# One 256-token tile's first layers: the high and low parts of its tokens laid side by side as one operand of 512 columns

## The chip, the cores and the metric

The kernel runs on one core of a Trainium2 chip. The time is the device time of the whole program in microseconds (us), the median of some executions. One further execution was recorded by the hardware profiler; its rows are quoted below.

The core's engines run side by side, each its own list of instructions in the order in which the program wrote it: PE (TensorE, matrix multiply; its weight loads are the rows PEld), DVE (VectorE), ACT (ScalarE), POOL (GpSimd), and SP, which issues the transfers. They wait for each other by semaphores. PE writes to eight accumulation banks of 128 x 512 numbers (PSUM), and DVE or ACT must read a bank out before PE may use it for something else.

## What is computed

```python
x  = attention(q, k, v)                    # 2304 tokens of 512 numbers
P  = sinkhorn(exp(x @ w_gate))             # 2304 x 8
for e in range(8):                         # 512 -> 1024 -> 512
    out += P[:, e:e+1] * (relu(x @ w1[e]) @ w2[e])
r  = relu(out @ w_in)                      # 512 -> 2048
y  = (r * r) @ w_out                       # 2048 -> 512
```

All of it is in float32. The kernel multiplies with operands of a shorter form (`F32R`) and keeps the accuracy by splitting each number in a high part and a low part: a product is hi x hi + hi x lo + lo x hi, three matmuls.

## The kernel before

After the attention (up to some 126 us) the work is a list of 80 steps. A step handles 256 hidden columns. Steps 0 to 31 are the eight experts for the first part of the tokens and 32 to 63 the experts again for the rest; steps 64 to 71 and 72 to 79 are the last two lines of the reference in the same manner. In steps 0 to 31 and 64 to 71 the first part of the tokens is a pair of tiles of 512 tokens and one single tile of 256 tokens; in the other steps there is a pair alone.

In a step, `l1_pair` makes the first layer of the pair in seven units u1 to u7 (a unit is a function that writes some 1.4 us of PE work), `l2_units` the second layer of the step before in eight units for the pair and two for the single tile, and `l1_single` the first layer of the single tile, at the end of the step's list `order`. The order written by hand is u1 u2 u3 u4, then a unit of layer two and one of u5 u6 u7 in turn, then the rest of layer two, then the single tile. `run(u)` calls a unit and then whatever was put down for its place: `after(k, f)` puts f down for k units later, and `prep_w` puts down the splitting of the next weights (ACT copies the high part, L159, and DVE subtracts, L163). `narrow` turns one quarter of a block of 64-bit weights into float32 in a few DVE instructions (L274 to L296); its stages are written behind fixed places of `order` (2, 16, 17 and 1) in steps 2 to 29.

Names for the steps of the argument:

- `xs` holds the single tile's tokens, the high parts `xs_hi` and the low parts `xs_lo`, each 4 pieces (kc) of 128 x 256.
- `l1_single` makes, for each of two groups of 128 hidden columns (fc) and each kc, three matmuls of 256 columns (L754): hi weights by `xs_hi`, hi weights by `xs_lo`, lo weights by `xs_hi`. From step 3 on both fc share one bank `mm`, of which there are three, and are one unit.
- `evac_g` empties it into `sg`: in the expert steps ACT takes relu (L608) and DVE the low part (L601); in steps 64 to 71 there are four instructions (relu, square, high part, low part).
- In `l1_pair`, u1 is copied from bank `s` to bank `pt` by ACT (L705); u4 adds to `pt`, which ACT copies to `s2` (L717); only then may u5 add to `pt`, which ACT copies to `s3` (L721). DVE adds bank `xt` to `s3` (L722), after which u7 may add to `xt`.

```python
        def u4():
            product(bank_b, i, "sum", 1, 5)
            after(0, lambda: nc.scalar.copy(made["s2"], bank_b))

        def u5():
            product(bank_b, i, "sum", 2, 6)
            after(0, lambda: nc.scalar.copy(made["s3"], bank_b))
```

Of the kernel before, what the change touches and what calls it, by code (L numbers as in the profile page):

```python
# [10 lines left out]
F32 = mybir.dt.float32  # L11
F32R = mybir.dt.float32r
# [3 lines left out]
ALU = mybir.AluOpType  # L16
# [15 lines left out]
KC = DM // 128  # L32
FB = 256
FC = FB // 128
NCH = NTOK // 128
SPE = FE // FB
NS1 = E * SPE
NS2 = FF // FB
T = 512
NSG = 256  # L40
PAIRS = (0, 1280)
SINGLE = 1024
SCALED = 3
# [5 lines left out]
def tile_kernel(ctx: ExitStack, tc: tile.TileContext, a):  # L49
    nc = tc.nc  # L50
    out = a["out"]

    const = ctx.enter_context(tc.tile_pool(name="const", bufs=1))
    big = ctx.enter_context(tc.tile_pool(name="big", bufs=1))
# [11 lines left out]
    const.tile([128, 96], F32, name="pad_x")  # L66
    x_hi = big.tile([128, 7, 2, T], F32R, name="x_hi")
    x_lo = big.tile([128, 7, 2, T], F32R, name="x_lo")
    xs = big.tile([128, 4 + 2 * KC * NSG], F32R, name="xs")
    xs_hi, xs_lo = (xs[:, 4:].rearrange("p (h k n) -> p h k n", h=2, n=NSG)[:, h] for h in range(2))  # L70
    ptile = big.tile([128, NCH, E], F32, name="ptile")
    big.tile([128, 104], F32, name="pad_w")

    xf = xfp.tile([128, KC, NTOK], F32, name="xf")

# [14 lines left out]
    bufs = {"s": 2, "xt": 2, "pt": 1, "mm": 3}  # L90

    def bank(tag):
        return psum.tile([128, 512], F32, tag=tag, name=tag, bufs=bufs[tag])

    post = [None]

    def tmp(name):
        return post[0].tile([128, 512], F32, tag="tmp", name=name, bufs=3)
# [6 lines left out]
    wset = [None, None]  # L105
# [454 lines left out]
    g_t, acc = {}, {}  # L560
    turned = []
    gbuf, block, r32, own, l2_banks, spare = [], {}, [], {}, [], []
# [14 lines left out]
    def after(k, f):  # L577

        due.setdefault(clock[0] + k, []).append(f)
# [14 lines left out]
    def evac_g(i, ghi, glo, src, k):  # L594

        moe, s = steps[i]
        n = src.shape[-1]

        def low(z, relu):
            if relu:  # L600
                nc.vector.scalar_tensor_tensor(  # L601
                    out=glo, in0=z, scalar=0.0, in1=ghi.bitcast(F32), op0=ALU.max, op1=ALU.subtract
                )
            else:
                nc.vector.tensor_tensor(out=glo, in0=z, in1=ghi.bitcast(F32), op=ALU.subtract)

        if moe:
            after(k, lambda: nc.scalar.activation(out=ghi, in_=src, func=AF.Relu))  # L608
            after(k + 1, lambda: low(src, True))
            return  # L610
        held = {}

        def square():
            held["r"] = tmp("r")[:, :n]
            nc.scalar.activation(out=held["r"], in_=src, func=AF.Relu)

        def product():
            held["g"] = tmp("g")[:, :n]
            nc.vector.scalar_tensor_tensor(
                out=held["g"], in0=src, scalar=0.0, in1=held["r"], op0=ALU.max, op1=ALU.mult  # L620
            )

        after(k, square)
        after(k + 1, product)
        after(k + 2, lambda: nc.scalar.copy(ghi, held["g"]))
        after(k + 3, lambda: low(held["g"], False))
# [109 lines left out]
        return [u1, u2, u3, u4, u5, u6, u7]  # L736

    def l1_single(i):
        whole = []

        def unit(fcs):

            if fcs[0] == 0:
                whole[:] = [sg[:, h].rearrange("p (f n) -> p f n", f=FC) for h in range(2)]
                g_t[i, 1] = {(f, 0): tuple(z[:, f] for z in whole) for f in range(FC)}
            gh, gl = whole
            ps = (spare[0] if i == 2 * NS1 else bank("mm"))[:, :len(fcs) * NSG]
            hi, lo = wset[i % 2]["blk"]
            for n, fc in enumerate(fcs):
                k = 0  # L750
                for kc in range(KC):
                    c = slice((4 * fc + kc) * 128, (4 * fc + kc) * 128 + 128)
                    for w, z in ((hi, xs_hi), (hi, xs_lo), (lo, xs_hi)):
                        nc.tensor.matmul(  # L754
                            ps[:, n * NSG:n * NSG + NSG], w[:, c], z[:, kc], start=k == 0, stop=k == 3 * KC - 1
                        )
                        k += 1
            gh, gl = (g[:, fcs[0]:fcs[-1] + 1].rearrange("p f n -> p (f n)") for g in (gh, gl))
            evac_g(i, gh, gl, ps, 0)

        if i >= SCALED:
            return [lambda: unit(list(range(FC)))]
        return [lambda fc=fc: unit([fc]) for fc in range(FC)]

    def l2_units(i, which):

# [138 lines left out]
    with tc.manual_schedule():  # L905
# [7 lines left out]
        ps = psum.tile([128, 512], F32, tag="s", name="s")  # L913
# [158 lines left out]
        sg = post[0].tile([128, 2, FC * NSG], F32R, name="sg", bufs=1)  # L1072
# [32 lines left out]
        for i in range(len(steps) + 1):  # L1105
# [16 lines left out]
            l1 = l1_pair(i) if i else first_units  # L1122
            order = l1[:4] if i else l1[2:4]
            l1s = l1_single(i) if pair_of(i) == 0 else []
            if mixed(i - 1):
                v = l2_mixed(i - 1)
# [24 lines left out]
            if i + 1 in first[1:]:  # L1151
                c = first[1:].index(i + 1)
# [116 lines left out]
```

## Time and profile before

| | us |
|---|---|
| median of 3 executions | 1944.39 (1944.38 to 1948.22) |
| the profiled execution | 1944.46 |
| its span, first to last instruction | 1942.7 |
| PE busy | 1921.6 (99%) |
| DVE busy | 1627.4 (84%) |
| ACT busy | 747.0 (38%) |
| POOL busy | 636.5 (33%) |

The time of an execution is 1.8 us more than the span, which lies before the first and behind the last instruction. A row of the trace reads: start in us from the span's start, length in us, engine, line of the kernel, operation, what it writes <- what it reads, shape; in brackets how long the engine stood idle before it, and for whom. The end of a PE row is modelled and overlaps the next row, so the distance from one start to the next tells what a matmul costs. Rows of DVE and ACT also overlap a little: the next one starts some 0.1 us before the last ends.

### The profile page before, as it was taken

Reading aid. Unit: us, or ns where it says so; the run is one execution under the profiler, and the core shown is the slowest. Engines: PE = TensorE matmul, PEld = TensorE weight load, DVE = VectorE, ACT = ScalarE, POOL = GpSimd, SP = SyncE. Lnnn points to the kernel's source line nnn. Section 1 sums busy time; section 2 is a strip of 40 time slices with the busy share of each in tenths; the row PEclk is TensorE's granted clock in tenths of the full one; section 3 lists DMA queues with packets and bytes.
Section 4 is the critical chain, followed back from the end, with each engine's and each line's share of the span. In section 5 each row is a group of like instructions: output and inputs, shape, how many; then the busy total and the mean of one; then the engine's idle time right before and its main releaser. Section 6 shows DMA issues by size and latency. Waiting matters only on the chain.

```text
span 1942.7 us, 29441 instructions
## 1 busy us (share of the span) xinstructions
PE 1921.6 (99%) x11050; PEld 1601.8 (82%) x11050; DVE 1627.4 (84%) x2337; ACT 747.0 (38%) x1238; POOL 636.5 (33%) x556
## 2 busy tenths in 40 slices
PE   8999999999999999999999999999999999999999
PEld 7778888888888888888888888888888878888887
DVE  5868888888888888888578999998999987785897
ACT  3544433333333333333243333433333355443443
POOL 4633332333432223333033332423233343331231
PEclk9999999999999999999999999999999999999999
DMA  7655776766666656556977676667566777779661
GB/s 263 212 217 201 275 270 243 266 253 243 237 260 260 239 227 249 222 220 247 382 288 266 249 268 250 255 258 269 200 260 249 301 289 262 263 277 394 227 250 66
DMA packets 166399, 491.84 MB, mean 253 GB/s; under 512 B 17248, under 2 KB 40176, under 8 KB 166256
## 3 DMA queue, kind: packets, MB, share of 16 engines
q1 hardware_dynamic: 166256, 489.96, 67.6%
q8 instruction: 87, 1.43, 0.3%
q14 instruction: 56, 0.46, 0.1%
HBM read 281.15 MB, written 208.74 MB: 252 GB/s over the span
## 4 chain that ended last, share of the span: by engine, by line
PE 94%; DVE 4%; issue 1%; ACT 1%; DMA 0%; POOL 0%; SPq 0%; DVEq 0%; ACTq 0%; POOLq 0%
PE mm L783 28%; PE pt L570 16%; PE s L570 11%; PE xt L570 11%; PE mm L866 10%; PE mm L754 6%; PE s L866 4%; PE xt L866 4%; PE xt L443 1%; PE mm L976 1%; PE s L391 1%; DVE acc L880 1%; PE pt L428 1%; DMA w2l<-w_w2l 0%; PE mm L477 0%
## 5 line engine op out<-in xcount | busy, mean ns | idle before, releaser
L783 PE MATMUL mm<-w2h,g 128*128 128x512 f32 x1312 | 405.7, 391 | 0.0
L805 DVE SCALAR_TENSOR_TENSOR acc<-mm,ptile,acc 128x512 f32<-128x512 f32 x290 | 216.8, 748 | 104.1 <-PE mm L783 103.8
L783 PEld LDWEIGHTS mm<-w2h,g 128*128 128x128 f32 x1312 | 245.0, 188 | 49.9
L783 PE MATMUL mm<-w2l,g 128*128 128x512 f32 x656 | 255.5, 390 | 0.0
L682 POOL TENSOR_TENSOR r<-mix,r 128x512 f32<-128x512 f32 x39 | 51.2, 1313 | 541.6 <-DVE mix L671 428.8
L653 DVE TENSOR_TENSOR g<-r,g 128x512 fp32r<-128x512 f32 x156 | 158.6, 1017 | 47.2 <-ACT g L650 45.5
L177 POOL TENSOR_TENSOR sums<-raw 128x256 f32<-128x256 f32 x40 | 32.7, 819 | 489.3 <-DVE suml L163 446.1
L650 ACT CAST g<-r 128x512 fp32r<-128x512 f32 x156 | 96.8, 621 | 130.2 <-PE mm L866 109.7
L880 DVE TENSOR_TENSOR acc<-mm,acc 128x512 f32<-128x512 f32 x226 | 144.7, 682 | 0.0
L783 PEld LDWEIGHTS mm<-w2l,g 128*128 128x128 f32 x656 | 123.2, 188 | 25.8
L570 PE MATMUL s<-x_hi,blkh 128*128 128x512 f32 x320 | 125.4, 392 | 1.1 <-ACT pt L705 1.1
L570 PE MATMUL pt<-x_hi,sumh 128*128 128x512 f32 x320 | 124.9, 390 | 0.6 <-ACT s L717 0.6
L570 PE MATMUL xt<-x_hi,sumh 128*128 128x512 f32 x320 | 124.8, 390 | 0.0
L570 PE MATMUL s<-x_lo,blkh 128*128 128x512 f32 x320 | 124.8, 390 | 0.0
L570 PE MATMUL s<-x_hi,blkl 128*128 128x512 f32 x320 | 124.7, 390 | 0.0
L570 PE MATMUL xt<-x_hi,suml 128*128 128x512 f32 x320 | 124.6, 389 | 0.0
L570 PE MATMUL pt<-x_lo,sumh 128*128 128x512 f32 x320 | 124.6, 389 | 0.0
L570 PE MATMUL pt<-x_hi,suml 128*128 128x512 f32 x320 | 124.6, 389 | 0.0
L570 PE MATMUL xt<-x_lo,sumh 128*128 128x512 f32 x320 | 124.6, 389 | 0.0
L608 ACT ACTIVATE sg<-mm 128x512 fp32r<-128x512 f32 (+1 forms) x35 | 19.7, 562 | 272.8 <-PE mm L754 272.8
L754 PE MATMUL mm<-xs,blkh 128*128 128x256 f32 x640 | 115.8, 280 | 0.0
L608 ACT ACTIVATE g<-s 128x512 fp32r<-128x512 f32 x96 | 59.6, 621 | 136.5 <-DVE s L722 69.1
(224 smaller groups left out, 4810.7 us busy)
## 6 DMA issues: line engine op xcount, KB each, us to landing
raw<-in_w SPq DMA_DIRECT2D x61, 512.0 KB, 6.3
blkh<-w_blkh SPq DMA_DIRECT2D x41, 512.0 KB, 3.6
blkl<-w_blkl SPq DMA_DIRECT2D x41, 512.0 KB, 4.4
sumh<-w_sumh SPq DMA_DIRECT2D x41, 512.0 KB, 4.7
suml<-w_suml SPq DMA_DIRECT2D x41, 512.0 KB, 5.7
w_blkh<-blkh SPq DMA_DIRECT2D x40, 512.0 KB, 6.1
w_blkl<-blkl SPq DMA_DIRECT2D x40, 512.0 KB, 6.5
w_sumh<-sumh SPq DMA_DIRECT2D x40, 512.0 KB, 6.5
```

The lines of the kernel that those rows point to most:

```text
L177: tt(out=c(sums, 0), in0=c(raw1, 2), in1=c(raw1, 3), op=ALU.add)
L391: nc.tensor.matmul(ps[QB * head:QB * head + QB, 2 * (g % 3) + g // 3, :], qt[rows, pr, g * QB:g * QB + QB], kt[rows, pr, g * QB:g * QB + K ...
L570: nc.tensor.matmul(ps, w[:, c], z[:, x, j], start=start and k == 0, stop=stop and k == 5, skip_group_check=True)
L608: after(k, lambda: nc.scalar.activation(out=ghi, in_=src, func=AF.Relu))
L650: after(k, lambda: nc.scalar.copy(b[:, 0], src))
L653: lambda: nc.vector.tensor_tensor(out=b[:, 1], in0=src, in1=b[:, 0].bitcast(F32), op=ALU.subtract),
L682: sub = lambda o, x, y: nc.gpsimd.tensor_tensor(out=o, in0=x, in1=y, op=ALU.subtract)
L754: nc.tensor.matmul(ps[:, n * NSG:n * NSG + NSG], w[:, c], z[:, kc], start=k == 0, stop=k == 3 * KC - 1)
L783: nc.tensor.matmul(ps, g[:, c0 * 128:c0 * 128 + 128], wt[:, fc], start=k == 0, stop=k == 3 * FC - 1)
L805: nc.vector.scalar_tensor_tensor(out=dst, in0=ps, scalar=p, in1=dst, op0=ALU.mult, op1=ALU.add)
L866: nc.tensor.matmul(ps, w[wt][:, c], z[:, g], start=start and k == 0, stop=stop and k == 2, skip_group_check=True)
L880: nc.vector.tensor_tensor(out=o, in0=ps, in1=o, op=ALU.add)
```

## The change

`xs` is laid out so that for each kc the high and the low part stand side by side: one operand of 512 columns. For steps 0 to 31 and 65 to 71, each fc is now a unit of its own with a bank of its own. For each kc there is one matmul of 512 columns, hi weights by both parts, and one of 256, lo weights by `xs_hi`, which adds to the bank's left half. The product is then the sum of the two halves: ACT copies the right half to `s3` (256 columns), and DVE adds the left half to it. `s3` is the same buffer that `l1_pair` uses. When both fc are done, `evac_g` reads `s3` instead of the bank, and is put down two units later than before. Step 64 keeps its three matmuls, in `one_bank`. Two spare columns move from `xs` to `pad_w`.

```diff
--- before.py
+++ after.py
@@ -66,10 +66,10 @@
     const.tile([128, 96], F32, name="pad_x")
     x_hi = big.tile([128, 7, 2, T], F32R, name="x_hi")
     x_lo = big.tile([128, 7, 2, T], F32R, name="x_lo")
-    xs = big.tile([128, 4 + 2 * KC * NSG], F32R, name="xs")
-    xs_hi, xs_lo = (xs[:, 4:].rearrange("p (h k n) -> p h k n", h=2, n=NSG)[:, h] for h in range(2))
+    xs = big.tile([128, KC, 2, NSG], F32R, name="xs")
+    xs_hi, xs_lo = (xs[:, :, h] for h in range(2))
     ptile = big.tile([128, NCH, E], F32, name="ptile")
-    big.tile([128, 104], F32, name="pad_w")
+    big.tile([128, 108], F32, name="pad_w")
 
     xf = xfp.tile([128, KC, NTOK], F32, name="xf")
 
@@ -736,31 +736,53 @@
         return [u1, u2, u3, u4, u5, u6, u7]
 
     def l1_single(i):
-        whole = []
-
-        def unit(fcs):
-
-            if fcs[0] == 0:
-                whole[:] = [sg[:, h].rearrange("p (f n) -> p f n", f=FC) for h in range(2)]
-                g_t[i, 1] = {(f, 0): tuple(z[:, f] for z in whole) for f in range(FC)}
-            gh, gl = whole
-            ps = (spare[0] if i == 2 * NS1 else bank("mm"))[:, :len(fcs) * NSG]
+        whole, halves = [], []
+
+        def set_out():
+            whole[:] = [sg[:, h].rearrange("p (f n) -> p f n", f=FC) for h in range(2)]
+            g_t[i, 1] = {(f, 0): tuple(z[:, f] for z in whole) for f in range(FC)}
+
+        def flat(h):
+            return whole[h].rearrange("p f n -> p (f n)")
+
+        def columns(fc, kc):
+            return slice((4 * fc + kc) * 128, (4 * fc + kc) * 128 + 128)
+
+        def one_bank():
+            set_out()
             hi, lo = wset[i % 2]["blk"]
-            for n, fc in enumerate(fcs):
-                k = 0
-                for kc in range(KC):
-                    c = slice((4 * fc + kc) * 128, (4 * fc + kc) * 128 + 128)
-                    for w, z in ((hi, xs_hi), (hi, xs_lo), (lo, xs_hi)):
-                        nc.tensor.matmul(
-                            ps[:, n * NSG:n * NSG + NSG], w[:, c], z[:, kc], start=k == 0, stop=k == 3 * KC - 1
-                        )
-                        k += 1
-            gh, gl = (g[:, fcs[0]:fcs[-1] + 1].rearrange("p f n -> p (f n)") for g in (gh, gl))
-            evac_g(i, gh, gl, ps, 0)
-
-        if i >= SCALED:
-            return [lambda: unit(list(range(FC)))]
-        return [lambda fc=fc: unit([fc]) for fc in range(FC)]
+            for fc in range(FC):
+                terms = [(kc, w, z) for kc in range(KC) for w, z in ((hi, xs_hi), (hi, xs_lo), (lo, xs_hi))]
+                for k, (kc, w, z) in enumerate(terms):
+                    nc.tensor.matmul(
+                        spare[0][:, fc * NSG:fc * NSG + NSG], w[:, columns(fc, kc)], z[:, kc],
+                        start=k == 0, stop=k == len(terms) - 1,
+                    )
+            evac_g(i, flat(0), flat(1), spare[0], 0)
+
+        def unit(fc):
+            if fc == 0:
+                set_out()
+                halves[:] = [post[0].tile([128, FC * NSG], F32, tag="s3", name="s3", bufs=1)]
+            ps = bank("mm")
+            hi, lo = wset[i % 2]["blk"]
+            for kc in range(KC):
+                nc.tensor.matmul(
+                    ps, hi[:, columns(fc, kc)], xs[:, kc].rearrange("p h n -> p (h n)"),
+                    start=kc == 0, stop=False, skip_group_check=True,
+                )
+                nc.tensor.matmul(
+                    ps[:, :NSG], lo[:, columns(fc, kc)], xs_hi[:, kc],
+                    start=False, stop=kc == KC - 1, skip_group_check=True,
+                )
+            pre = halves[0][:, fc * NSG:fc * NSG + NSG]
+
+            after(0, lambda: nc.scalar.copy(pre, ps[:, NSG:]))
+            after(1, lambda: nc.vector.tensor_tensor(out=pre, in0=ps[:, :NSG], in1=pre, op=ALU.add))
+            if fc == FC - 1:
+                evac_g(i, flat(0), flat(1), halves[0], 2)
+
+        return [one_bank] if i == 2 * NS1 else [lambda fc=fc: unit(fc) for fc in range(FC)]
 
     def l2_units(i, which):
 
```

Line numbers move with it (L805 is L827 now, L809 is L831). The order of the instructions changes at three places.

ACT at the end of an expert step and the start of the next, before; `mm_4971` is the single tile's bank, `s_4999` and `pt_5000` are banks of the next step's `l1_pair`:

```order
L159 CAST mixh1_2268<-mix32_2266 128x1024
L608 ACTIVATE sg_2265<-mm_4971 128x512
L705 COPY pt_5000<-s_4999 128x512
L159 CAST w2h1_2259<-raw2_109 128x1024
L159 CAST blkh0_137<-raw1_107 128x1024
L608 ACTIVATE g1_2264<-s_4999 128x512
L717 COPY s2_5025<-pt_5000 128x512
```

ACT at the same place now; `mm_4939` and `mm_4951` are the two banks of the single tile, `s3_4938` the buffer of the sums:

```order
L159 CAST mixh1_2268<-mix32_2266 128x1024
L780 COPY s3_4938<-mm_4939 128x256
L780 COPY s3_4938<-mm_4951 128x256
L705 COPY pt_4963<-s_4962 128x512
L608 ACTIVATE sg_2265<-s3_4938 128x512
L159 CAST w2h1_2259<-raw2_109 128x1024
L159 CAST blkh0_137<-raw1_107 128x1024
L608 ACTIVATE g1_2264<-s_4962 128x512
L717 COPY s2_4989<-pt_4963 128x512
```

Two copies are new, and the relu into `sg` has moved behind L705, just ahead of the two weight copies; it now reads what DVE wrote.

DVE at the same place, before:

```order
L805 SCALAR_TENSOR_TENSOR acc1_2262<-mm_4960,ptile_85,acc1_2262 128x512
L274 TENSOR_SCALAR xb_4968<-xb_4826 128x512
L278 SCALAR_TENSOR_TENSOR xb_4968<-xb_4826,xb_4968 128x512
L282 TENSOR_SCALAR xb_4826<-xb_4826 128x512
L285 SCALAR_TENSOR_TENSOR xb_4968<-xb_4826,xb_4968 128x512
L601 SCALAR_TENSOR_TENSOR sg_2265<-mm_4971,sg_2265 128x512
L289 TENSOR_SCALAR xb_4826<-xb_4968 128x512
L292 SCALAR_TENSOR_TENSOR xb_4826<-xb_4826 128x512
L296 TENSOR_TENSOR xb_4968<-xb_4968,xb_4826 128x512
L163 TENSOR_TENSOR w2l1_2260<-raw2_109,w2h1_2259 128x1024
```

DVE at the same place now:

```order
L827 SCALAR_TENSOR_TENSOR acc1_2262<-mm_4927,ptile_85,acc1_2262 128x512
L274 TENSOR_SCALAR xb_4935<-xb_4793 128x512
L278 SCALAR_TENSOR_TENSOR xb_4935<-xb_4793,xb_4935 128x512
L282 TENSOR_SCALAR xb_4793<-xb_4793 128x512
L285 SCALAR_TENSOR_TENSOR xb_4935<-xb_4793,xb_4935 128x512
L781 TENSOR_TENSOR s3_4938<-mm_4939,s3_4938 128x256
L781 TENSOR_TENSOR s3_4938<-mm_4951,s3_4938 128x256
L289 TENSOR_SCALAR xb_4793<-xb_4935 128x512
L292 SCALAR_TENSOR_TENSOR xb_4793<-xb_4793 128x512
L296 TENSOR_TENSOR xb_4935<-xb_4935,xb_4793 128x512
L601 SCALAR_TENSOR_TENSOR sg_2265<-s3_4938,sg_2265 128x512
L163 TENSOR_TENSOR w2l1_2260<-raw2_109,w2h1_2259 128x1024
```

The two additions stand behind the four `narrow` instructions L274 to L285, and the low part into `sg` has moved behind the next three.

DVE at the start of step 72, before: the rows `acc0` are the pair's layer two of step 71, and the rows `acc1` that of the single tile, which reads `sg`:

```order
L619 SCALAR_TENSOR_TENSOR g_15266<-mm_15227,r_15252 128x512
L809 TENSOR_TENSOR acc0_2261<-mm_15268,acc0_2261 128x512
L809 TENSOR_TENSOR acc0_2261<-mm_15278,acc0_2261 128x512
L605 TENSOR_TENSOR sg_2265<-g_15266,sg_2265 128x512
L809 TENSOR_TENSOR acc0_2261<-mm_15288,acc0_2261 128x512
L809 TENSOR_TENSOR acc0_2261<-mm_15297,acc0_2261 128x512
L809 TENSOR_TENSOR acc1_2262<-mm_15306,acc1_2262 128x512
```

The same place now:

```order
L619 SCALAR_TENSOR_TENSOR g_15197<-s3_15142,r_15186 128x512
L831 TENSOR_TENSOR acc0_2261<-mm_15199,acc0_2261 128x512
L831 TENSOR_TENSOR acc0_2261<-mm_15209,acc0_2261 128x512
L605 TENSOR_TENSOR sg_2265<-g_15197,sg_2265 128x512
L831 TENSOR_TENSOR acc1_2262<-mm_15219,acc1_2262 128x512
```

The low part into `sg` now stands behind the last `acc0` row, with no unit of the pair left between it and the matmuls that read it.

## Rows read from the trace of the kernel before

**Rows 1.** The page: busy time by engine, and the chain that ended last.

```profile
PE 1921.6 (99%) x11050; PEld 1601.8 (82%) x11050; DVE 1627.4 (84%) x2337; ACT 747.0 (38%) x1238; POOL 636.5 (33%) x556
...
PE 94%; DVE 4%; issue 1%; ACT 1%; DMA 0%; POOL 0%; SPq 0%; DVEq 0%; ACTq 0%; POOLq 0%
```

**Rows 2.** Timeline of PE, end of step 15 and start of step 16.

```profile
521.27 0.40 PE L754 MATMUL mm<-xs,blkh 128*128 128x256 f32 x2
...
524.12 0.40 PE L570 MATMUL s<-x_hi,blkh 128*128 128x512 f32 x1
...
529.35 0.39 PE L570 MATMUL pt<-x_hi,suml 128*128 128x512 f32 x1
...
530.93 0.39 PE L570 MATMUL pt<-x_hi,sumh 128*128 128x512 f32 x1
```

**Rows 3.** Timeline of ACT, the same place and a little later.

```profile
524.38 0.60 ACT L608 ACTIVATE sg<-mm 128x512 fp32r<-128x512 f32 x1 [9.03 <-PE mm L754]
525.70 0.57 ACT L705 COPY pt<-s 128x512 f32<-128x512 f32 x1 [0.71 <-PE s L570]
526.18 1.06 ACT L159 CAST w2h<-raw 128x1024 fp32r<-128x1024 f32 x1
527.12 1.05 ACT L159 CAST blkh<-raw 128x1024 fp32r<-128x1024 f32 x1
528.41 0.60 ACT L608 ACTIVATE g<-s 128x512 fp32r<-128x512 f32 x1 [0.23 <-PE s L570]
529.77 0.59 ACT L717 COPY s<-pt 128x512 f32<-128x512 f32 x1 [0.76 <-PE pt L570]
...
535.95 0.63 ACT L608 ACTIVATE g<-s 128x512 fp32r<-128x512 f32 x1 [2.87 <-DVE s L722]
536.49 0.58 ACT L608 ACTIVATE g<-pt 128x512 fp32r<-128x512 f32 x1
536.97 0.61 ACT L311 CAST pp<-pp 128x512 fp32r<-128x512 f32 x1
```

**Rows 4.** Timeline of DVE, the same place.

```profile
523.18 0.99 DVE L274 TENSOR_SCALAR xb<-xb 128x512 int32<-128x512 int32 x1
...
527.28 0.68 DVE L601 SCALAR_TENSOR_TENSOR sg<-mm,sg 128x512 fp32r<-128x512 f32 x1
527.88 0.41 DVE L289 TENSOR_SCALAR xb<-xb 128x512 int32<-128x512 int32 x1
...
535.24 0.68 DVE L722 TENSOR_TENSOR s<-xt,s 128x512 f32<-128x512 f32 x1
```

**Rows 5.** Groups of DVE by form: an operation on 256 columns.

```profile
L601 DVE SCALAR_TENSOR_TENSOR sg<-mm,sg 128x256 fp32r<-128x256 f32 x6 | 2.4, 412 | 0.8 <-ACT sg L608 0.8
```

**Rows 6.** Timelines of DVE: L274 at another step, then L601 in two steps.

```profile
263.38 0.41 DVE L274 TENSOR_SCALAR xb<-xb 128x512 int32<-128x512 int32 x1
...
241.49 0.68 DVE L601 SCALAR_TENSOR_TENSOR sg<-mm,sg 128x512 fp32r<-128x512 f32 x1
...
266.88 0.68 DVE L601 SCALAR_TENSOR_TENSOR sg<-mm,sg 128x512 fp32r<-128x512 f32 x1
```

**Rows 7.** Timelines of POOL beside the two L274 rows above, the earlier step first.

```profile
263.35 1.03 POOL L181 TENSOR_TENSOR sums<-sums,raw 128x256 f32<-128x256 f32 x1
...
523.15 0.74 POOL L181 TENSOR_TENSOR sums<-sums,raw 128x256 f32<-128x256 f32 x1
```

**Rows 8.** Timelines at the start of step 30: DVE, then PE.

```profile
893.75 0.68 DVE L601 SCALAR_TENSOR_TENSOR sg<-mm,sg 128x512 fp32r<-128x512 f32 x1
...
894.65 0.39 PE L570 MATMUL pt<-x_hi,sumh 128*128 128x512 f32 x1
```

**Rows 9.** Timelines in step 72: DVE, then PE.

```profile
1771.18 0.68 DVE L605 TENSOR_TENSOR sg<-g,sg 128x512 fp32r<-128x512 f32 x1
...
1773.29 0.69 DVE L809 TENSOR_TENSOR acc<-mm,acc 128x512 f32<-128x512 f32 x1 [0.67 <-PE mm L783]
...
1773.09 0.62 PE L783 MATMUL mm<-w2h,sg 128*128 128x512 f32 x2
```

## The prediction

> **What bounds the kernel now.** I read the page first. PE is busy for 99% of the span and holds 94% of the chain that ended last [rows 1]: whatever makes PE's list shorter shortens the time, and whatever makes PE wait lengthens it. DVE at 84% and ACT at 38% count only where PE waits for them, so the second view is the timeline at the place of the change, the end of one step and the start of the next. I take step 15 into 16; steps repeat every 25.98 us.
>
> PE there stands never still. The single tile's 24 matmuls of 256 columns start at 521.27 and u1 starts at 524.12, so one costs 2.85 / 24 = 118.8 ns; from there 23 matmuls of 512 columns later it is 529.35, so one of these costs 5.23 / 23 = 227.4 ns [rows 2]. Neither is twice the other: each matmul carries some 10 ns that do not depend on its columns. ACT waits most of the time, but not between L705 and L717: it makes two weight copies and a relu there, and the last thing in front of u5 is L717, which ends at 529.77 + 0.59 = 530.36; u5 starts at 530.93 [rows 2, 3]. So u5 has 0.57 us to spare. DVE comes to the single tile late: the bank is ready at 524.4, when ACT reads it [rows 3], but DVE's L601 follows only at 527.28, behind `narrow` [rows 4]. Before the change nothing on PE's path waits for that lateness.
>
> **What the change takes from PE.** For each fc and kc, three matmuls of 256 become one of 512 and one of 256: 2 x 118.8 - 227.4 = 10.2 ns less. Eight of these in 39 steps (0 to 31 and 65 to 71) make 39 x 8 x 10.2 = 3.2 us. The columns are the same, so it is only the fixed part of 312 matmuls. The Trainium skill (TensorE: Matmul & The Clock Gate, Back-to-back issue gap) puts the distance between warm matmuls at N / 2.4 + 2.5 ns, by which a pair of 256 joined to one of 512 saves only 2.5 ns, 0.8 us in all; the rows show more, and the measured distance decides. By the page the sum below would be 2.4 us higher.
>
> **What it adds, and where that is hidden.** Two copies of 256 columns on ACT a step: ACT stood idle for 9.03 us before this place [rows 3], so they cost nothing. Two additions on DVE: an operation on 256 columns takes 0.41 us [rows 5], 0.33 from start to start, as one of 0.68 takes 0.60 [rows 4]. The second bank: both are free again when the additions end at about 528, and the units of layer two that reuse them start after 532, so no bank is waited for.
>
> **The wait that it makes.** The relu into `sg` used to wait for PE alone. Now it reads `s3`, so it waits for both additions, and these stand in DVE's list behind `narrow`'s L274 to L285. On ACT the two weight copies, the relu of u3 and L717 are queued behind that relu, and u5 waits for L717. L705 stands ahead of it and is not delayed. Step 15 into 16, worked through:
>
> DVE is free at 527.28, where L601 started [rows 4]. First addition 0.33, second 0.41: 528.02. Hand-over to ACT 0.03, as from L722 (535.24 + 0.68 = 535.92) to the relu at 535.95 [rows 3, 4]. A relu reading SBUF takes 0.54 to the next start, a weight copy 0.94 (taken for both), a relu reading a bank 0.48 [rows 3]: 528.05 + 0.54 + 0.94 + 0.94 + 0.48 = 530.95 for L717's start, 531.54 for its end, 531.57 for PE. Without the wait u5 would start at 530.93 less the 0.08 saved, 530.85. **PE waits 0.72 us**, more than eight times what the step saves. The wait comes back in each step, since DVE stands idle for PE again in the middle of every step and so starts the next end of a step where it started this one.
>
> How often: 27 steps (2 to 28) have `narrow` at this place. In 19 of them L601 starts as late as here; the first is at 241.49, and 11 x 25.98 later is 527.27. In six it starts 0.6 us earlier, the first at 266.88 [rows 6], and there PE waits only 0.12. The other two, the first of all, leave nothing. The difference is L274, which takes 0.41 or 0.99 us, as POOL's L181 beside it takes 1.03 or 0.74 [rows 4, 6, 7]: they start within 0.03 us of each other, and one waits for the other. The Trainium skill (SBUF — State Buffer, SBUF: two separate sides) calls this an exclusive lock, which whichever of the two starts first keeps for its whole instruction, and the rows agree: one of the two is always long. The change moves neither of them, so I keep 19 and six: 19 x 0.72 + 6 x 0.12 = 14.4 us. If all were long it would be 27 x 0.72 = 19.4, if all 25 were short 3.0.
>
> **Step 30.** At the end of step 29 `settled` writes the last stage of `narrow` too ahead of step 30, so DVE is free only at 893.75, while u5 starts at 894.65 [rows 8]. The first addition stands before that stage and the second behind it, so the chain is the same 4.29 us: 898.04 against 894.57. **PE waits 3.5 us**, once.
>
> **Step 72.** Layer two of step 71 runs here at once. The low part into `sg` was done at 1771.18 + 0.68; now it stands behind the accumulation of the pair's last unit before the single tile, at 1773.29 [rows 9]. From there, 0.08 earlier: 1773.21 + 0.60 + 0.68 + 0.03 = 1774.52. The second matmul of the single tile reads it and would start at 1773.09 - 0.08 + 0.23 = 1773.24. **PE waits 1.3 us**, once. At step 32 three units lie between, and nothing waits.
>
> **Steps 65 to 71 and 0 to 2.** No `narrow` stands there in steps 65 to 71, so the additions follow at once, but the high part into `sg` now precedes L717. Nothing to 0.54 us a step, 0 to 3.8 in all; I take nothing, because u5 has 0.57 to spare in the step shown. In steps 0 and 1 DVE works on the routing probabilities instead; 0 to 0.7 us each, taken as nothing.
>
> **The sum.** -3.2 + 14.4 + 3.5 + 1.3 = +16.0 us. The profiled execution took 1944.46, 0.07 more than the median: 1960.5.
>
> **The rivals.**
> First, nothing on PE waits: the relu into `sg` gets its sums in time and the change gives what it takes from PE, 1944.5 - 3.2 = 1941.2. It decides if ACT has 0.72 us more to spare than I count, or DVE comes to the additions before 526.6. For it speaks that ACT is busy for only 38%; against it that the relu stands ahead of both weight copies, and that DVE's row starts at 527.28. Half of it, L274 always short, still leaves 1944.5 - 3.2 + 3.0 + 3.5 + 1.3 = 1949.1.
>
> Second, DVE itself becomes late for PE. L722 must end before u7 may add to `xt`. It ended at 535.92; the additions put 0.66 before it, and the low part into `sg` now reads two operands in SBUF. That makes 536.6 to 537.0, against u7 at 24 matmuls after u5, 536.38, moved to 537.02 by the wait at u5. It is just covered. If POOL holds L289 as it held L274, another 0.58 is lost and some 0.3 us a step is waited for on top: 27 x 0.3 = 8, 1968.6.
>
> Third, the rest of steps 0 to 2 and 65 to 71 costs its upper ends: 3.8 + 1.4, 1965.7.
>
> **Chances.** The forecast, with its own spread by L274 and by 0.1 us a step of error in the chain (2.7 us): 0.72. DVE too late: 0.08. The outer steps: 0.07. Nothing waits: 0.13. The range goes from L274 always short, 1949, to DVE too late, 1968; it leaves out the case in which nothing waits and a little at the top. A change of 0.2% (3.9 us) is about what a measurement of this kernel can tell from none. A saving of 3.2 us at most lies within that: faster 0.02, same 0.11, slower 0.87.
>
> **What would show it.** Right: the waits of PE name L717 (ACT, into `s2`) as the longest, about 0.7 us some 20 times and 3.5 once; steps of 26.6 us instead of 25.98 between 235 and 880; in step 72 a wait for L605 of 1.3 us; the new matmuls at 227 and 119 ns. Wrong: steps of 25.9, with ACT's relu into `sg` starting before 526.6 on the same scale; or waits of PE at u7 for L722; or L274 short, or long, in nearly all steps.

## The result, and the profile after

The changed kernel takes 1974.82 us (median of 5 runs, 1967.67 to 1975.35), against 1946.6 for the kernel before beside it (1944.38 to 1948.22): a ratio of 1.0142, interval 1.0126 to 1.0158. The profiled execution took 1974.82, 30.4 us more than that of before (1944.46); the medians just given lie 28.2 apart. The direction was forecast, the size was not: 1960.5 was predicted, and the time lies above the range. Of the 30.4 us the prediction had named 16.

The page of the changed kernel, busy time by engine and the chain that ended last, answers to [rows 1]; under it are the first rows of TensorE's waits (us in total, times, longest):

```profile
PE 1935.1 (98%) x10738; PEld 1587.3 (80%) x10738; DVE 1657.8 (84%) x2412; ACT 767.9 (39%) x1313; POOL 638.9 (32%) x556
...
PE 77%; DVE 14%; issue 5%; ACT 4%; POOL 0%; ACTq 0%; DVEq 0%; POOLq 0%
```

```profile
PE pt L570 <- ACT s L717: 15.1, 27, 2.9
...
PE mm L529 <- DVE scs L523: 2.9, 3, 1.4
PE mm L770 <- DVE acc L827: 2.5, 1, 2.5
...
PE mm L805 <- DVE sg L605: 1.2, 1, 1.2
```

PE has 312 matmuls fewer and is still named busy for 13.5 us more. Of these 8.0 lie in the 25 steps described below: what a matmul loses behind a wait counts as busy, and so does a part of the wait itself, because the modelled end of the row ahead reaches into it (0.47 us idle in the row of step 16 below, where the start comes 0.62 late). Another 2.8 lie in the attention phase. DVE holds 14% of the chain where it held 4%. The wait for L717 was 0.6 us in all and is 15.1; the waits for L827 and L605 are new, and the one for L827 stood in no term of the prediction. The wait for L523, a sum that DVE makes for the routing probabilities, was 1.9 and is 2.9.

**One step.** The end of step 15 and the start of step 16, PE first, to be read against [rows 2]; then ACT against [rows 3], DVE and POOL against [rows 4, 7]:

```profile
532.09 0.39 PE L770 MATMUL mm<-xs,blkh 128*128 128x512 f32 x1
...
534.90 0.40 PE L570 MATMUL s<-x_hi,blkh 128*128 128x512 f32 x1
...
541.54 0.39 PE L805 MATMUL mm<-w2l,g 128*128 128x512 f32 x1
542.39 0.50 PE L570 MATMUL pt<-x_hi,sumh 128*128 128x512 f32 x1 [0.47 <-ACT s L717]
542.73 0.40 PE L570 MATMUL pt<-x_lo,sumh 128*128 128x512 f32 x1
...
543.89 0.62 PE L805 MATMUL mm<-w2h,g 128*128 128x512 f32 x2
```

```profile
538.85 0.63 ACT L608 ACTIVATE sg<-s 128x512 fp32r<-128x512 f32 x1 [1.78 <-DVE s L781]
539.39 1.04 ACT L159 CAST w2h<-raw 128x1024 fp32r<-128x1024 f32 x1
540.34 1.04 ACT L159 CAST blkh<-raw 128x1024 fp32r<-128x1024 f32 x1
541.28 0.59 ACT L608 ACTIVATE g<-s 128x512 fp32r<-128x512 f32 x1
541.77 0.57 ACT L717 COPY s<-pt 128x512 f32<-128x512 f32 x1
```

```profile
534.00 0.99 DVE L274 TENSOR_SCALAR xb<-xb 128x512 int32<-128x512 int32 x1
...
538.08 0.74 DVE L781 TENSOR_TENSOR s<-mm,s 128x256 f32<-128x256 f32 x2
```

```profile
533.97 0.73 POOL L181 TENSOR_TENSOR sums<-sums,raw 128x256 f32<-128x256 f32 x1
```

The chain is the predicted one, link by link: the additions behind `narrow` (the row L781 x2 is both of them), the relu into `sg` 0.03 us behind them, two weight copies, the relu of u3, L717, u5. From the step's first single-tile matmul to u5 it is 542.39 - 532.09 = 10.30 us; before it was 530.93 - 521.27 = 9.66 [rows 2]. The difference, 0.64, is the predicted 0.72 less the 0.08 saved.

Three things beside it are not as predicted. The block of 16 matmuls takes 534.90 - 532.09 = 2.81 us, against 2.85 for the 24 before, and the ten matmuls behind it are slower than before by more than the 0.04 that it saves. The matmul behind the wait takes 542.73 - 542.39 = 0.34 us to the next start, and the six to 543.89 take 1.50 where six times 0.227 is 1.36: a wait costs **0.14 us** besides its own length. And L274 is long in every step: of all its rows from 235 to 880 us on each kernel (duration in ns, least, median, most), before and after:

```profile
L274 DVE TENSOR_SCALAR xb<-xb x25: 410/996/1000, 237.4 to 860.9; 128x512 int32<-128x512 int32 x25
```

```profile
L274 DVE TENSOR_SCALAR xb<-xb x24: 990/994/995, 239.6 to 855.2; 128x512 int32<-128x512 int32 x24
```

The 25th of the changed kernel starts at 881.9 and takes 0.99 too.

The 25 steps from 237.71 to 906.80 (ends of steps 4 to 28) take 26.76 us each, where they took 25.98: **19.6 us** of the 30.4.

**Step 30** answers to [rows 8]; below the PE rows stands the view by windows (length, PE busy and matmuls, granted clock, DMA share, GB/s):

```profile
916.25 0.39 PE L805 MATMUL mm<-w2l,g 128*128 128x512 f32 x1
919.52 0.71 PE L570 MATMUL pt<-x_hi,sumh 128*128 128x512 f32 x1 [2.89 <-ACT s L717]
920.03 0.63 PE L570 MATMUL pt<-x_lo,sumh 128*128 128x512 f32 x1
...
923.02 0.41 PE L805 MATMUL mm<-w2l,g 128*128 128x512 f32 x1
```

```profile
912.00:916.20 4.20, 4.20 (x20) 1.00 0.01 4
919.50:923.00 3.50, 3.48 (x8) 0.52 0.82 329
923.00:927.00 4.00, 4.00 (x19) 0.99 0.95 307
```

u5 would follow at 916.47; it starts at 919.52, a wait of 3.05 (predicted 3.5). Then eight matmuls take 3.50 us where 8 x 0.227 is 1.81: the granted clock is 0.52 over these 3.50 us, so nearly all of them ran at the lower of the two levels (1.2 GHz), and it was 1.00 before the wait. The step is longer by 4.8.

**The end of step 30** holds the wait that the prediction had excluded, first PE, then DVE:

```profile
938.85 0.28 PE L774 MATMUL mm<-xs,blkl 128*128 128x256 f32 x1
941.58 0.50 PE L770 MATMUL mm<-xs,blkh 128*128 128x512 f32 x1 [2.46 <-DVE acc L827]
```

```profile
937.03 1.22 DVE L163 TENSOR_TENSOR suml<-sums,sumh 128x1024 fp32r<-128x1024 f32 x1
938.17 0.42 DVE L289 TENSOR_SCALAR xb<-xb 128x512 int32<-128x512 int32 x1
938.62 1.11 DVE L292 SCALAR_TENSOR_TENSOR xb<-xb 128x512 f32<-128x512 uint32 x1
939.76 1.10 DVE L296 TENSOR_TENSOR xb<-xb 128x512 f32<-128x512 f32 x1
940.78 0.74 DVE L827 SCALAR_TENSOR_TENSOR acc<-mm,ptile,acc 128x512 f32<-128x512 f32 x1
```

The second fc needs a bank that layer two filled just before. Its accumulation L827 stands in DVE's list behind a weight's low part and three instructions of `narrow`, which in this step lie at the end of the step. The step is longer by 2.7.

**Step 72** [rows 9], DVE, then PE:

```profile
1802.70 0.68 DVE L605 TENSOR_TENSOR sg<-g,sg 128x512 fp32r<-128x512 f32 x1
```

```profile
1803.44 0.50 PE L805 MATMUL mm<-w2h,sg 128*128 128x512 f32 x1 [1.16 <-DVE sg L605]
```

The matmul ahead starts at 1801.89, so this one would at 1802.12: a wait of 1.32 (predicted 1.3).

**Step 1**, DVE, before and after, holds a wait that the prediction took as nothing:

```profile
134.14 0.42 DVE L523 TENSOR_REDUCE scs<-ptile 128x8 f32<-128x144 f32 x1
...
140.50 0.41 DVE L523 TENSOR_REDUCE scs<-ptile 128x8 f32<-128x144 f32 x1
```

```profile
134.62 0.41 DVE L523 TENSOR_REDUCE scs<-ptile 128x8 f32<-128x144 f32 x1
134.95 0.68 DVE L601 SCALAR_TENSOR_TENSOR sg<-s,sg 128x512 fp32r<-128x512 f32 x1
...
142.01 0.41 DVE L523 TENSOR_REDUCE scs<-ptile 128x8 f32<-128x144 f32 x1
```

The low part into `sg` used to be made ahead of the first of these two L523 and now stands between them. The second comes 7.39 us behind the first instead of 6.36, and PE waits for it. From the first block of single-tile matmuls to the next it is 30.40 us instead of 29.39.

### The profile page after: what moved, and what is told of

It is laid out like the page before. It is cut to its first block, busy times and chain, and to the rows that moved or that the text cites. A ratio compares the mean times of both kernels' runs of the same rounds, so it can differ in the third digit from the quotient of the medians.

```text
span 1973.0 us, 28998 instructions
## 1 busy us (share of the span) xinstructions
PE 1935.1 (98%) x10738; PEld 1587.3 (80%) x10738; DVE 1657.8 (84%) x2412; ACT 767.9 (39%) x1313; POOL 638.9 (32%) x556
## 4 chain that ended last, share of the span: by engine, by line
PE 77%; DVE 14%; issue 5%; ACT 4%; POOL 0%; ACTq 0%; DVEq 0%; POOLq 0%
PE mm L805 22%; PE pt L570 15%; PE mm L888 10%; PE xt L570 9%; PE s L570 7%; PE s L888 4%; PE xt L888 4%; DVE acc L827 2%; DVE xb L278 2%; DVE xb L285 2%; PE xt L443 1%; ACT w2h L159 1%; DVE xb L274 1%; DVE suml L163 1%; DVE xb L282 1%
## 5 line engine op out<-in xcount | busy, mean ns | idle before, releaser
L805 PE MATMUL mm<-w2h,g 128*128 128x512 f32 x1312 | 406.3, 391 | 0.0
L827 DVE SCALAR_TENSOR_TENSOR acc<-mm,ptile,acc 128x512 f32<-128x512 f32 x290 | 216.5, 747 | 107.4 <-PE mm L805 107.1
L805 PEld LDWEIGHTS mm<-w2h,g 128*128 128x128 f32 x1312 | 245.3, 188 | 50.6
L805 PE MATMUL mm<-w2l,g 128*128 128x512 f32 x656 | 255.4, 389 | 0.0
L805 PEld LDWEIGHTS mm<-w2l,g 128*128 128x128 f32 x656 | 123.3, 188 | 26.0
L570 PE MATMUL pt<-x_hi,sumh 128*128 128x512 f32 x320 | 128.3, 401 | 15.1 <-ACT s L717 15.1
L780 ACT COPY s<-mm 128x256 f32<-128x256 f32 x78 | 29.0, 372 | 286.7 <-PE mm L774 284.7
L770 PE MATMUL mm<-xs,blkh 128*128 128x512 f32 x312 | 111.6, 398 | 2.5 <-DVE acc L827 2.5
```

Source lines behind the costliest of these rows:

```text
L570: nc.tensor.matmul(ps, w[:, c], z[:, x, j], start=start and k == 0, stop=stop and k == 5, skip_group_check=True)
L770: nc.tensor.matmul(ps, hi[:, columns(fc, kc)], xs[:, kc].rearrange("p h n -> p (h n)"), start=kc == 0, stop=False, skip_group_check=True,)
L805: nc.tensor.matmul(ps, g[:, c0 * 128:c0 * 128 + 128], wt[:, fc], start=k == 0, stop=k == 3 * FC - 1)
L827: nc.vector.scalar_tensor_tensor(out=dst, in0=ps, scalar=p, in1=dst, op0=ALU.mult, op1=ALU.add)
```

## The experiments

Before and changed kernel differ by some us from run to run in the attention phase, ahead of the steps: the first single-tile block started between 119.6 and 129.9 us in the profiled runs. So small effects are read from the length of a step in the trace, from one step's first single-tile matmul to the next one's.

**The two kernels again** (no edit), to see what a second profile repeats.

> The kernel before once more, for its profile. In the first profile 20 of the first 28 L274 were long (0.99 us) and eight short; in the changed kernel and in its four variants all are long but the first two. If chance decides each time which of L274 and POOL's L181 goes first, this profile again has a mixture, with other steps short. If the place in the program decides it, the same steps are short. Steps of 25.98 us either way.

> The changed kernel once more, for its profile; its five runs lay at 1967.7 and 1972.3 to 1975.4. If L274 is long in nearly all steps again, the time is 1972 to 1976 and the steps are 26.76 us; each step in which it is short should be 0.6 us shorter, so a run of 1968 would have some ten of them. If it is a mixture as in the kernel before, about 1970.

Measured: 1941.59 and 1976.9. Before again: steps of 25.98, L274 short in two of the 25 steps, other steps than in the first profile, which had six. After again: all long, steps of 26.78. So the six short ones belong to no place in the program; each profile of the kernel before deals them anew. In the changed kernel there is nothing to deal: in both its profiles, and in those of the nine runs below other than the one with the small POOL instruction, all 25 are long.

**The copy for w2 behind L717**

```diff
-                at = ... else (1, 3, 6, 7, 13, 15)
+                at = ... else (5, 7, 6, 7, 13, 15)
```

> The changed kernel with one weight copy (w2, ACT L159, and its DVE partner) put down four units later in the expert steps, so that it no longer stands between the relu into sg and L717. My theory (PE waits for L717, which is queued on ACT behind a relu that waits for DVE's additions): the chain to u5 gets 0.95 us shorter, which is more than the 0.73 us of the wait, so some 25 waits of 0.86 us (the wait and the slow restart behind it) go: 1974.8 - 21.5 = 1953. Step 30 keeps about 2 of its 3 us. Rival (DVE simply has too much to do, ACT's order is no matter): within 2 us of 1975.

Measured: 1949.54 (1946.15 to 1957.06), ratio 1.0037 (1.0020 to 1.0055). ACT's rows show the edit, L717 is ahead of the copy into `w2h`:

```profile
525.08 0.58 ACT L717 COPY s<-pt 128x512 f32<-128x512 f32 x1
525.54 1.06 ACT L159 CAST w2h<-raw 128x1024 fp32r<-128x1024 f32 x1
```

None of the 25 steps waits at u5, though L274 stays long, and they are 25.99 us. The edit moves DVE's low part of w2 as well, but the additions come as late as before it, 5.99 us behind the step's first single-tile matmul with the edit and without. So the queue on ACT makes the wait together with DVE's lateness: taking one 0.94 us copy out of it is enough. The waits of the steps 30 (2.1 us now), 30 into 31, and 72 stay.

**GpSimd's second sums one place later**

```diff
-            out += [..., (4 if spread else 1, s2), ...]
+            out += [..., (4 if spread else 2 if 3 < n < NS1 else 1, s2), ...]
```

> The changed kernel with one edit: GpSimd's second pair of sums one place later from step 3 on, so that it no longer starts beside VectorE's L274; w2's copy stays ahead of u5's. If L274's 0.99 us beside GpSimd's L181 is what sets the wait at u5, L274 takes 0.41 in all steps, u5's operand comes 0.58 us sooner, TensorE's wait there falls from 0.56 to under 0.1 us, and the steps are 26.0 to 26.2 us long, the time 1956 to 1962. If it is w2's copy ahead of it on ScalarE alone, or VectorE is caught by GpSimd in the next place just as long, the steps stay at 26.7 and the time at 1972 to 1976.

Measured: 1974.8 (1972.32 to 1976.56), ratio 1.0158 (1.0144 to 1.0173), as the changed kernel. It tells nothing between the theories: POOL's list is the same with either place, since nothing else of POOL's stands between, and L181 starts as before (POOL, then DVE, at one step):

```profile
536.58 0.73 POOL L181 TENSOR_TENSOR sums<-sums,raw 128x256 f32<-128x256 f32 x1
```

```profile
536.61 0.99 DVE L274 TENSOR_SCALAR xb<-xb 128x512 int32<-128x512 int32 x1
```

**One small POOL instruction ahead of these sums**

```diff
             def s2():
+                if 3 < n < NS1:
+                    nc.gpsimd.memset(pad_x[:, :8], 0.0)
                 tt(out=c(sums, 1), in0=c(sums, 0), in1=c(raw1, 0), op=ALU.subtract)
```

> The changed kernel with one edit: GpSimd sets eight columns of an unused buffer to zero ahead of its second pair of sums (L181), from step 3 on, so that L181 starts some tens of ns behind VectorE's L274 instead of 20 ns ahead of it. In the one step in which L181 came 33 ns behind, L274 took 0.41 us. If the order of these two starts decides L274's length, and that the wait at u5, L274 takes 0.41 in the 25 steps, TensorE's wait for L717 falls from 0.56 to under 0.15 us a step, the steps are 25.99 to 26.2 us long, and the time 1956 to 1961. If w2's copy ahead of u5's alone makes the wait, or another place catches VectorE as long, the steps stay at 26.7 and the time at 1972 to 1977.

Measured: 1958.28 (1955.2 to 1962.79), ratio 1.0069 (1.0050 to 1.0088). POOL, DVE, and all 25 steps (L181 is L183 here, L274 is L276):

```profile
531.53 0.10 POOL L182 MEMSET pad_x<- 128x8 f32 x1
531.60 0.98 POOL L183 TENSOR_TENSOR sums<-sums,raw 128x256 f32<-128x256 f32 x1
```

```profile
531.57 0.41 DVE L276 TENSOR_SCALAR xb<-xb 128x512 int32<-128x512 int32 x1
...
L276 DVE TENSOR_SCALAR xb<-xb x25: 410/410/411, 242.9 to 872.2; 128x512 int32<-128x512 int32 x25
```

An instruction of 0.10 us on an engine that is idle two thirds of the time takes 14 us off the 25 steps; the medians differ by 16.5. POOL now comes 16 to 25 ns behind L274 in all 25 steps, and L274 is short in all. The steps are 26.18 to 26.20 in 21 and 26.38 or 26.39 in four: the wait at u5 that is left is 0.05 us and costs 0.14 more. Here POOL catches L289 instead (1.00 us). In the four longer steps u7 too waits, 0.04 to 0.07 us for DVE's L722 (L724 here), which is the prediction's second rival.

**The additions ahead of `narrow`**

```diff
-                stages = {2: 0, 16: 1, 17: 2, 1: 3}
+                stages = {2: 0, 16: 1, 0: 2, 1: 3}
```

> The changed kernel with narrow's second stage (L282, L285) written behind the first unit of the next step instead of behind place 17, so that DVE makes both additions before it and nothing else changes. My theory (the additions come late because narrow stands ahead of them): they come 1.9 us earlier, the waits for L717 go except in step 30: 1974.8 - 21.5 = 1953. Rival 1 (DVE has too much to do): no change, 1975, since DVE does the same work up to L722. Rival 2 (DVE late at L722, the wait that was covered by the one at u5): up to 0.3 us come back at u7 in steps with a long L296, 4 to 8 us in all, 1957 to 1961.

Measured: 1955.64 (1951.74 to 1957.94), ratio 1.0054 (1.0040 to 1.0068). Steps of 25.99 without a wait at u5, as DVE is there in time. In four steps the prediction's second rival shows in the waits, for u7; by the starts of the matmuls it is 0.41 us each, and these steps are 26.53 to 26.55 long:

```profile
PE xt L570 <- DVE s L722: 1.0, 4, 0.2
```

The two special waits of the steps 30 and 30 into 31 come with the lower clock here and cost 4.8 and 4.1.

**One bank, read directly, at the steps 29, 30 and 71**

```diff
+            ps = spare[0] if i == 2 * NS1 else bank("mm")
...
-        return [one_bank] if i == 2 * NS1 else ...
+        return [one_bank] if i in (NS1 - 3, NS1 - 2, 2 * NS1, first[3] - 1) else ...
```

> The changed kernel, but steps 29, 30 and 71 make the single tile's first layer as before the change (three matmuls into one bank, no additions). My theory: the 3 us wait at the start of step 30 with the slow clock behind it (4.8 together), the bank wait at the end of step 30 (2.7) and the wait in step 72 (1.4) go, 0.3 of saving is given back: 1974.8 - 8.6 = 1966. Rival (the steps around 30 are slow for another reason, DVE being behind): 1972 to 1975.

Measured: 1963.46 (1962.05 to 1965.98), ratio 1.0092 (1.0070 to 1.0113), 11 us under the changed kernel. L827 and L605 are gone from the waits, and the longest for L717 is a usual step's:

```profile
PE pt L570 <- ACT s L717: 12.2, 26, 0.6
```

**Left half only.** The hi weights by the low parts are left out: no copy, no additions, the relu reads the bank's left half, and the matmuls stay.

```diff
-            after(0, lambda: nc.scalar.copy(pre, ps[:, NSG:]))
-            after(1, lambda: nc.vector.tensor_tensor(out=pre, in0=ps[:, :NSG], in1=pre, op=ALU.add))
-            if fc == FC - 1:
-                evac_g(i, flat(0), flat(1), halves[0], 2)
+            evac_g(i, whole[0][:, fc], whole[1][:, fc], ps[:, :NSG], 0)
```

> The part on PE alone: the operand of 512 columns and a bank for each half of the hidden columns, but the right halves (hi weights by low tokens) are left out of the sum, so there is neither copy nor addition, and each bank is emptied at once by a relu and a subtraction. My theory: the matmuls save 39 x 0.086 = 3.3 us, no wait for L717 is left, and the wait of 2.6 us for a bank at the end of step 30, which comes from the second bank, stays: 1944.5 - 3.3 + 2.6 = 1944, and some 1 more if the starting steps keep theirs. Rival (the second bank or the long operand costs time in each step): 1950 or more.

Measured: 1947.4 (1942.24 to 1952.62), ratio 1.0013 (0.9999 to 1.0028). No new wait is left but the second bank's, and the steps are 25.99, not 25.90. So the saving is not hidden by a wait: PE itself does not give it.

**Order and address of the matmuls**, both on top of the later copy for w2: first the four of 512 ahead of the four of 256 in each bank, then the change's order with `xs` four columns into its buffer, as it lay before (the change moves four spare columns to `pad_w`, not two).

```diff
             for kc in range(KC):
                 nc.tensor.matmul(ps, hi[:, columns(fc, kc)], ...)
+            for kc in range(KC):
                 nc.tensor.matmul(ps[:, :NSG], lo[:, columns(fc, kc)], xs_hi[:, kc], ...)
```

```diff
-    xs = big.tile([128, KC, 2, NSG], F32R, name="xs")
+    xs_room = big.tile([128, 4 + KC * 2 * NSG], F32R, name="xs")
+    xs = xs_room[:, 4:].rearrange("p (k h n) -> p k h n", h=2, n=NSG)
```

> e1_copy_later with the matmuls of each bank in another order: first the four of 512 columns, then the four of 256. In e1 and e4 a step without waits takes 25.993 us against 25.980 before: a 512 that precedes a 256 takes 235 ns instead of 227, and the ten matmuls behind the block lose another 53 ns, so that the expected 0.086 us of saving is gone. If changing width at each matmul costs it: steps of 25.90 to 25.93 us here. If the long operand itself costs it, or something outside the block: 25.99 again.

> e1_copy_later with xs moved back to where it began before the change, four columns (16 bytes) into its buffer. If the address of the tokens costs the expected saving: steps of 25.90 us. If not (the order of widths does): 25.99, as in e1.

Measured: 1946.57 and 1949.81, one run each. Steps of 25.946 and 25.953 against 25.994 with the later copy alone and 25.98 before; blocks of 2.780 and 2.787 us against 2.810. Either gives about half of what is missing, where the expectations had nearly all of it or nothing.

**Mended.** The later copy with one bank at three steps; then both together with the grouped order and the old address.

> The changed kernel with the copy for w2 later and one bank at the steps 29, 30 and 71, but with the matmuls in the change's order and the tokens at its address. Against the run with all four edits it tells what order and address are worth: steps of 25.99 us expected, none of the waits, and a time of 0.5 to 1.5 us over the kernel before, 2 to 4 us over the run with all four. If order and address are worth nothing, the two agree within 1 us.

> The changed kernel with four edits: the copy and the subtraction for w2 at places 5 and 7 (no wait at u5), one bank straight to its evacuation at the steps 29, 30 and 71 (none of the three special waits), the four 512-column matmuls of a bank ahead of its four of 256, and the tokens four columns into their buffer as before. By my account of the loss all of it is then mended and a part of the saving is there: steps of 25.90 to 25.95 us against 25.98 before, no wait of TensorE at L717, L827 or L605, and a time 1 to 3 us under the kernel before. The rival, that the two-bank form costs something which none of the four edits touches (the busier ScalarE and VectorE), expects steps of 25.98 or more and a time level with before or above it.

Measured: 1945.46 (1940.98 to 1948.6), ratio 1.0010 (1.0001 to 1.0019), and **1940.83** (1938.71 to 1944.74), ratio 0.9985 (0.9977 to 0.9994). Of the waits for L717, L827 and L605 one of 0.6 us is left in either, as in the kernel before. Steps are 25.99 and 25.94: order and address together give 0.05, hardly more than either alone. The first is 2.1 us over the kernel before beside it (1943.39), where at most 1.5 was expected. In the second, PE at step 15:

```profile
521.10 1.09 PE L772 MATMUL mm<-xs,blkh 128*128 128x512 f32 x4
522.02 0.62 PE L777 MATMUL mm<-xs,blkl 128*128 128x256 f32 x4
522.48 1.08 PE L772 MATMUL mm<-xs,blkh 128*128 128x512 f32 x4
523.40 0.63 PE L777 MATMUL mm<-xs,blkl 128*128 128x256 f32 x4
523.87 0.40 PE L571 MATMUL s<-x_hi,blkh 128*128 128x512 f32 x1
```

The block takes 2.77 us: the 0.08 that the prediction counted are saved, and 0.04 are lost again in the twelve matmuls behind it. Of the 4.6 us between the two medians, 39 x 0.05 = 2 are the steps; another 1.6 lies ahead of the steps in the profiled runs, where runs differ anyway. This version beats the changed kernel, and by 0.15% the kernel before.

## Why the prediction was wrong

The mechanism was right: the wait for L717 from the relu's new place. What failed are sizes, terms put at nothing, and one sentence that excluded a wait. L274 always long alone would not have done it: the prediction had priced that at 19.4 us, which makes 1965.5. Above the range the time came by what the sum did not hold at all: the extra cost of each wait, the wait for the second bank, the lower clock in step 30 and the first steps. Of the 14.4 us by which the sum fell short:

| step of the prediction | forecast | measured | short by |
|---|---|---|---|
| "I keep 19 and six": L274 | six short steps | none | 6 x 0.60 = 3.6 |
| a wait costs its length | 0 | 0.14 in each of 25 steps | 3.5 |
| "no bank is waited for" | 0 | 2.7 | 2.7 |
| step 30, less the saving | 3.4 | 4.8 | 1.4 |
| "the other two ... leave nothing" | 0 | 0.7 | 0.7 |
| the saving in the 12 other steps | -1.0 | 0.1 | 1.1 |
| step 72, less the saving | 1.2 | 1.5 | 0.3 |
| steps 0 and 1, "taken as nothing" | 0 | 1.0 | 1.0 |
| attention | 0 | 0.5 | 0.5 |

These are 14.8; 0.5 goes off for waits of before between the steps 32 and 65 that are gone.

**The chance of L274.** This is the largest, by little. "The change moves neither of them" was true of the order in the program and false of the starts by some nanoseconds. In the profile of before, L181 started 29 or 30 ns ahead of L274 in ten steps, of which five had L274 short, and 23 to 27 ns ahead in 15, of which one had. In the second profile of before, two of 14 were short at 29 or 30 ns and none of the 11 nearer ones. In the changed kernel the lead is 20 to 27 ns in all 25, and none is short. The small POOL instruction turned the order round, and all were short: shown. The Trainium skill (SBUF — State Buffer, SBUF: two separate sides) gives the pair of ports that VectorE and GpSimd share to whichever starts first, for its whole instruction. The runs agree, except that a lead of 29 or 30 ns by these records did not decide it. The rows of the prediction had that already: L181 starts 0.03 us ahead both times, and L274 is short once and long once [rows 4, 6, 7]. What shifted the lead by some ns in the changed kernel stays open.

**The wait's extra cost.** The prediction added waits as gaps. The first matmul behind each takes 0.11 us longer and the next ones a little more, 0.14 in all. Rows of before showed it and were not read for it: the matmul at 195.47 would be followed at 195.70, so the next one waited 0.06 us, and the one after it followed 0.34 later, as here.

```profile
195.76 0.50 PE L570 MATMUL pt<-x_hi,blkh 128*128 128x512 f32 x1
196.10 0.40 PE L570 MATMUL pt<-x_lo,blkh 128*128 128x512 f32 x1
```

**The second bank.** The argument asked when the new banks are free again, not from whom they are taken. The bank that the second fc takes was layer two's, and at the end of step 30 its accumulation is late on DVE. One bank there took the wait away, and the run with the left half only, which has two banks and no additions, kept it (2.62 us): shown.

**Step 30.** The chain counted both additions behind the last stage of `narrow`; only the second is (0.42 at 915.54), so the wait was 3.05, not 3.5. The lower clock after it cost 1.7 more and stood in no term.

**The saving.** The forecast step was 2 x 118.8 - 227.4 = 10.2 ns a pair. It holds for matmuls among their like. In the changed kernel, alternating, a 512 ahead of a 256 takes 235 ns and a 256 ahead of a 512 116, and the matmuls behind the block give back 0.05. The alternation alone does not do it: with `xs` at its old address the same order takes 225 and 122 in most of the block. Order and address bring half of the saving back; why the rest is lost behind the block stays open. Under the waits it cost nothing, as u5 started when ACT let it.

**Steps 0 to 3.** At the end of step 2, u6 waited 0.58 for L721, as ACT's queue was late there too. The 1.0 in the steps 0 and 1 is the wait for L523 behind the low part into `sg`: at that place PE waits 1.56 us, 1.58 in the second profile of the changed kernel, but 0.62 in the first of before and 0.60 with the left half only, where `sg` is made at its old place. This is a part of the third rival, which the sum left out.

One reading of the prediction was off without harm: between L705 and L717 ACT does wait, 0.23 and 0.76 us [rows 3]. Right were the chain at u5 to 0.01 us, step 72, and that the steps 65 to 71 wait for nothing. Of the rivals, the first (nothing waits) is what the later copy makes of the 25 steps, and the second was seen in four steps each of the runs with the additions first and with the small POOL instruction.

## What to carry to other kernels

When a value moves from PSUM straight to a relu, to a sum that another engine makes first, look at what is queued behind the relu: here two weight copies stood between it and the operand that TensorE needed next, and moving one of them was worth 19 us in the 25 steps, 25 between the medians. For each new buffer or bank ask whose it was last, step by step, not only when it comes free again. A duration that has two values in a trace need not keep its mixture when something else changes: price both ends over all steps, and find out which start decides it.

## What was not expected of the hardware

Two engines' starts within 30 ns decide 0.58 us a step: an instruction of 0.10 us on GpSimd made VectorE's L274 0.41 us in 25 of 25 steps, and these steps 14 us shorter in all. After the wait of 3.05 us the granted clock was 0.52 for eight matmuls; after the wait of 2.6 us at the end of step 30 it was 1.00 in the same run, but low after a wait there in the second run of the same kernel (0.75 over 939.0 to 944.5). So the length of the wait alone did not decide it in these runs. And where the moving operand starts in its buffer, zero or four columns in, changed the block of 16 matmuls from 2.810 to 2.787 us, in one profile each, the same in all 25 steps.
